# A fused forward-and-backward block on one Trainium2 core: the first stage gets a written order of loads and turns

## The chip, the cores and the metric

The kernel runs on one core of one Trainium2 chip. The metric is the device time of one execution in microseconds. A core has five engines with a queue each, which they work off in the order in which the program was built: TensorE (PE; its weight loads are listed apart, as PEld), VectorE (DVE), ScalarE (ACT), GpSimd (POOL) and SyncE (SP), which here only issues transfers. Transfers (DMA) run on 16 engines that all queues share; SP issues the plain and the transposing ones, POOL the gathers and most stores.

## What is computed

The reference is the forward pass of a block and all its gradients. Cut to what matters:

```python
mod = (_silu(c) @ w_mod).reshape(c.shape[0], 6, 1, -1)
sa, ca, ga, sb, cb, gb = (mod[:, 0], ..., mod[:, 5])
h = _layernorm(x) * (1 + ca) + sa
x = x + ga * irfft2(rfft2(h) * (w_r + 1j * w_i))      # spectral mixer
h = _layernorm(x) * (1 + cb) + sb
z = _layernorm(h)                                     # MLP
x = x + gb * (gelu(z @ w1 + b1) @ w2 + b2)
...
_out, _vjp = jax.vjp(_f, A_x, A_w_r, A_w_i, B_w1, B_b1, B_w2, B_b2, c, w_mod)
_grads = _vjp(grad_out)
```

There are 2048 tokens of width 1024, a hidden width of 3584, and all inputs are bfloat16. The backward pass of the MLP needs (grad_out * gb) @ w2^T, which depends on no forward result: only on grad_out, on the row gb and on w2. The kernel calls this product `ph`.

## The kernel before

The first stage has four jobs.

- Rows of `mod`. `mod_block(r, h)` makes half h of row r: eight products of 128x512 (line 278) over a 1 MB tile of w_mod that `mod_load` brings (line 270), and one eviction out of PSUM (line 281). Row 5 is gb, row 1 is ca, row 0 the shift sa; the rows 2, 3 and 4 (`late_mods`) are needed later. Their tiles take turns in three buffers.
- grad_out turned and scaled. `load_go(j)` loads a quarter of 512 tokens (1 MB, line 350). For each quarter and each of eight column chunks four 128x128 products against an identity fill a PSUM tile `pt` (line 386), which DVE (even chunks, line 390) or ACT (odd chunks, line 394) evicts into `gBoT[j]`, multiplied by the column `gb_col`. That column comes out of the gb row by eight tiny products (line 378) and one copy (line 380).
- The product `ph`. `ph_part(fc, js)` makes, for 128 hidden units fc and the token quarters js, eight products of 128x512 each over `wt` and `gBoT[j]` (line 808), and one eviction (line 814); a complete fc is stored by POOL (line 816). `wt` holds two tiles of w2^T; `load_w2t(fg)` brings one, for two values of fc, as a transposing transfer of 0.5 MB (line 341). There are 28 values of fc, so 896 products, the last 64 of them behind the first MLP products. They depend on nothing but gb, grad_out and w2, so TensorE works on them wherever something else isn't ready.
- The spectral mixer's input. `load_tok` loads a quarter of x by one plain transfer on SP (line 143) and two gathers on POOL (line 145), 0.25 MB each. Then DVE and ACT make the layer norm (`ln_dve`, `ln_mix`, `norm_act`: lines 487, 497, 501, 504, 512), and DVE scales by 1 + ca and folds (line 194, all through the helper `tt`). The first products on the folded input are `pu` (line 535). Beside this POOL, DVE and ACT make tables of sines (`gen_mats`, `trig`: index products on POOL, line 416; a reduction on DVE, line 443; the sine on ACT, line 444), into buffers of which one is grad_out's second quarter (`smb`) and one its first (`px1`).

In the kernel before the loads stand in the order in which the lines 358 to 375 name them: ca first, then gb, grad_out, the first w2 tile, the other quarters of grad_out and of x. The products of the four row halves, the turns of all four quarters and then `ph` follow each other. A scheduler that places instructions by its own estimates decides what lies between what on each engine; `tc.issue_after(x)` puts a floor under it (not before x), and `tc.high_priority()` lets an eviction go ahead. What is built is a fixed order per engine.

After the spectral mixer the kernel makes a second and a third layer norm per quarter (`consume_fwd`, stored as `d_n3` on line 865), while TensorE works through a long run of `ph` products. Then the MLP begins with the products `pz` (line 937), whose evictions are ACT's (line 940). From the first `pz` on the order on TensorE is the same in both kernels.

Of the kernel before, what the change touches and what calls it, by code (L numbers as in the profile page):

```python
# [17 lines left out]
P = 128  # L18
# [17 lines left out]
def kernel(  # L36
# [104 lines left out]
    def load_tok(t4, src, i, eng=None):  # L141
        s3 = tok_flat(src)
        ins = (eng or nc.sync).dma_start(out=tok_plain(t4, i), in_=tok_rows(s3, i, 0, D))
        for q in range(2):
            nc.gpsimd.indirect_dma_start(out=t4[:, tok_idx(i, q), :], out_offset=None, in_=s3,
                                         in_offset=bass.IndirectOffsetOnAxis(ap=xidx[:, 2 * i + q:2 * i + q + 1], axis=0))
        return ins
# [120 lines left out]
    def mod_load(r, h, wblk, eng):  # L268
        cb = 2 * r + h
        eng.dma_start(out=wblk, in_=w_mod[:, cb * KH:(cb + 1) * KH].rearrange("(j p) n -> p j n", p=P))  # L270

    def mod_block(r, h, wblk=None):
# [4 lines left out]
        for jc in range(NDC):  # L277
            nc.tensor.matmul(pm[:], lhsT=u_b[:, jc, :], rhs=wblk[:, jc, :], start=(jc == 0), stop=(jc == NDC - 1))
# [3 lines left out]
        if r in (1, 4):  # L282
            nc.vector.tensor_scalar(out=dst, in0=dst, scalar1=1.0, scalar2=None, op0=ALU.add)

# [64 lines left out]
    def load_go(j):  # L349
        nc.sync.dma_start(out=gos[j], in_=go_f[j * BW:(j + 1) * BW, :].rearrange("(a p) d -> p a d", p=P))  # L350
# [3 lines left out]
    def mod_get(r, h):  # L354
        wm[r, h] = mod_tile()
        mod_load(r, h, wm[r, h][:], nc.sync)

    mod_get(1, 0)
    load_tok(x4s[0], A_x, 0)
    mod_get(1, 1)  # L360
    mod_get(5, 0)
    for h in range(2):
        mod_block(1, h, wm[1, h][:])
    mod_get(5, 1)
    load_go(0)
    load_w2t(0)
    load_go(1)
    load_tok(x4s[1], A_x, 1)
    load_go(2)
    load_go(3)  # L370
    for h in range(2):
        mod_block(5, h, wm[5, h][:])
    load_tok(x4s[2], A_x, 2)
    load_tok(x4s[3], A_x, 3)
    load_w2t(1)
    pc = ps_d("pc")
    for cch in range(NDC):
        nc.tensor.matmul(pc[:, cch:cch + 1], lhsT=gb_row[0:1, cch * P:(cch + 1) * P], rhs=ones_bf[0:1, 0:1], start=True, stop=True)
    with tc.high_priority():
        nc.vector.tensor_copy(out=gb_col[:], in_=pc[:, 0:NDC])  # L380
    for j in range(4):
        for cch in range(NDC):
            pt = ps_f("pt")
            for a in range(4):
                q = (0, 2, 3, 1)[a] if j % 2 == 0 else (1, 3, 2, 0)[a]
                nc.tensor.matmul(pt[:, q * P:(q + 1) * P], lhsT=gos[j][:, a, cch * P:(cch + 1) * P], rhs=(ident, irev)[a // 2],
                                 start=True, stop=True)
            if cch % 2 == 0:
                with tc.high_priority():
                    nc.vector.tensor_scalar(out=gBoT[j][:, cch, :], in0=pt[:], scalar1=gb_col[:, cch:cch + 1], scalar2=0.0,  # L390
                                            op0=ALU.mult, op1=ALU.add, accum_out=gu[:, j, cch:cch + 1])
            else:
                with tc.high_priority():
                    nc.scalar.activation(out=gBoT[j][:, cch, :], in_=pt[:], func=ACT.Identity, scale=gb_col[:, cch:cch + 1],
                                         accum_out=gu[:, j, cch:cch + 1])
# [18 lines left out]
    def pts(out, in0, s1, s2, o0, o1=None):  # L414
        kw = {} if o1 is None else {"op1": o1}
        nc.gpsimd.tensor_scalar(out=out, in0=in0, scalar1=s1, scalar2=s2, op0=o0, **kw)
# [18 lines left out]
    def trig(dst, colv, rowv, nrow, width, modn, cosine):  # L435
# [3 lines left out]
        for r in range(nrow):  # L439
            ov = idx[:, r * width:(r + 1) * width]  # L440
            pts(ov.rearrange("p (s w) -> p s w", s=2) if len(colv.shape) == 3 else ov, colv, rowv[r], sh, ALU.mult, ALU.add)
# [3 lines left out]
                             bias=negpi[:], scale=2 * np.pi / modn)  # L445

# [4 lines left out]
    def gen_mats():  # L451
        for cl, colv, modn in ((CE, kev, 2048), (SE, kev, 2048), (CO, kod, 4096), (SO, kod, 4096)):
# [4 lines left out]
            for r in range(0, n, 2):  # L457
                trig(sm[:, cl // 2, r:r + 2, :], colv, rows[r:r + 2], 2, 512, modn, cl < 2)
            nc.gpsimd.dma_start(out=d_SF[:, cl, 0:n], in_=sm[:, cl // 2])
# [335 lines left out]
    pho = reg.tile([P, 3, 4, BW], BF16, name="pho", tag="ot")  # L795
    phs = [pho[:, k] for k in range(3)] + [reg.tile([P, 4, BW], BF16, name="phr", tag="ph")[:]]
    last_pe = [None]

    def ordered():
        return tc.issue_after(last_pe[0].ins)  # L800

    def ph_part(fc, js):
        fg, k = fc // 2, fc % 2
        ph2 = phs[fc % 4]
        for j in js:
            pp = ps_f("pp")
            for cch in range(NDC):
                last_pe[0] = nc.tensor.matmul(pp[:], lhsT=wt[:, fg % 2, cch, k * P:(k + 1) * P], rhs=gBoT[j][:, cch, :],  # L808
                                              start=(cch == 0), stop=(cch == NDC - 1))
            q = (0, 2, 3, 1)[j]  # L810
            ov = ph2[:, :, q * P:(q + 1) * P]
            pv = pp[:, :].rearrange("p (i w) -> p i w", w=P)
            with tc.high_priority():
                nc.any.tensor_copy(out=ov, in_=pv)  # L814
        if js[-1] == 3:
# [735 lines left out]
```

## Time and profile before

| what | before |
|---|---|
| median of 3 runs | 1419.64 us (1416.66 to 1420.49) |
| profiled execution, its own time | 1419.22 us |
| span of its profile | 1417.4 us |
| busy PE, DVE, ACT, POOL | 1367.5, 1071.1, 745.6, 377.1 us |
| bytes moved | 333.22 MB |
| granted TensorE clock, mean | 0.99 |

In a timeline row stand the start, the busy time, the engine and line, the operation with its output and inputs, the number of instructions merged in the row, and in brackets the idle time before it with what ended it. A windows row gives for one stretch the busy time of each engine with the instruction count, then the granted clock of TensorE, the mean busy share of the 16 DMA engines, and GB/s.

### The profile page before, as it was taken

How to read it: one execution, taken by the hardware profiler on the slowest of the kernel's cores; microseconds unless marked ns; L12 is line 12 of the kernel's file. 1: busy time of each engine (PE TensorE's matmuls, PEld its weight loads, DVE VectorE, ACT ScalarE, POOL GpSimd, SP SyncE). 2: the span in 40 equal slices, each digit the busy share in tenths (PEclk: the TensorE clock that was granted, in tenths of full speed). 3: DMA queues.
4: the chain of work that ended last, by engine and by line, in shares of the span. 5: the costliest groups of instructions: out<-in, count | busy, mean ns of one | idle time of the engine just before them, and what ended most of it. 6: DMA issues, size and time to landing. Idle time of an engine off the chain costs nothing. (4 is left out here: it accounts for less than half of the span.)

```text
span 1417.4 us, 18569 instructions
## 1 busy us (share of the span) xinstructions
PE 1367.5 (96%) x6839; PEld 663.0 (47%) x6963; DVE 1071.1 (76%) x1503; ACT 745.6 (53%) x1063; POOL 377.1 (27%) x479
## 2 busy tenths in 40 slices
PE   5999999999999999999999999999999999999998
PEld 2545675444444444444444444344544565444443
DVE  5898889987698877886520788999488659898642
ACT  4775667667887765666315583343623445343211
POOL 5500623201112122212210011011367432322332
PEclk8899999999999999999999999999999999999999
DMA  9972647899688776687999399996699997666993
GB/s 330 304 226 72 181 137 226 261 277 348 239 235 267 231 252 233 200 275 232 292 287 233 115 271 319 210 298 193 191 279 281 242 242 207 189 180 182 288 261 118
DMA packets 356689, 333.22 MB, mean 235 GB/s; under 512 B 207578, under 2 KB 297200, under 8 KB 356470
## 3 DMA queue, kind: packets, MB, share of 16 engines
q1 hardware_dynamic: 319110, 205.61, 55.1%
q0 software_dynamic: 37488, 126.42, 25.7%
q8 instruction: 54, 0.88, 0.3%
q14 instruction: 37, 0.30, 0.1%
HBM read 166.77 MB, written 115.92 MB: 199 GB/s over the span
## 5 line engine op out<-in xcount | busy, mean ns | idle before, releaser
L808 PE MATMUL pp<-gBoT,wt 128*128 128x512 bf16 x874 | 196.3, 381 | 4.0 <-DMA wt<-in_B_w_dram 2.8
L1094 PE MATMUL pg<-w1T,gzr 128*128 128x512 bf16 x877 | 195.0, 379 | 3.7 <-ACT gn3b L1109 1.7
L1445 PE MATMUL gw1acc<-gzh,n3n 128*128 128x512 bf16 x877 | 194.1, 379 | 1.0
L1094 PEld LDWEIGHTS <-gzr 128*128 128x128 bf16 x896 | 86.4, 98 | 110.8 <-issue 7.9
L808 PEld LDWEIGHTS <-wt 128*128 128x128 bf16 x896 | 87.6, 98 | 107.5 <-DMA wt<-in_B_w_dram 3.3
L937 PEld LDWEIGHTS <-w 128*128 128x128 bf16 x896 | 87.1, 98 | 107.4 <-issue 2.7
L1445 PEld LDWEIGHTS <-n3n 128*128 128x128 bf16 x896 | 87.2, 98 | 105.2 <-issue 1.3
L937 PE MATMUL pz<-n3Ta,w 128*128 128x512 bf16 x439 | 98.2, 379 | 1.8 <-ACT gt L940 1.3
L937 PE MATMUL pz<-n3Tb,w 128*128 128x512 bf16 x436 | 98.0, 379 | 0.7 <-issue 0.2
L940 ACT ACTIVATE gt<-pz,b_col 128x512 bf16<-128x512 f32 x112 | 73.5, 684 | 38.1 <-PE pz L937 37.6
L994 PEld LDWEIGHTS <-hhA 128*128 128x128 bf16 x608 | 58.9, 98 | 73.4 <-issue 3.0
L1227 PE MATMUL gw2acc<-gB,hhsA 128*128 128x512 bf16 x406 | 91.2, 379 | 0.5
L1449 ACT CAST gwo<-gw1acc 128x512 bf16<-128x512 f32 x49 | 28.5, 582 | 111.0 <-PE gw1acc L1445 103.2
L194 DVE TENSOR_TENSOR gt<-gt,gt 128x2048 bf16<-128x2048 bf16 x56 | 68.5, 1224 | 20.6 <-ACT gt L953 19.4
L951 ACT ACTIVATE gt<-gt 128x2048 bf16<-128x2048 bf16 x28 | 53.5, 1910 | 55.1 <-DVE gt L194 55.1
L194 DVE TENSOR_TENSOR ct<-ct 128x2048 bf16<-128x2048 bf16 x68 | 80.8, 1217 | 1.4 <-DMA d_n<-ct 0.5
L1234 ACT CAST gwo<-gw2acc 128x512 bf16<-128x512 f32 x46 | 26.7, 582 | 101.0 <-PE gw2acc L1227 83.2
L1227 PEld LDWEIGHTS <-hhsA 128*128 128x128 bf16 x416 | 40.6, 98 | 47.9
L947 ACT ACTIVATE gt<-gt 128x2048 bf16<-128x2048 bf16 x28 | 53.5, 1910 | 1.7 <-DVE w2sA L194 1.0
L1450 POOL DMA_DIRECT2D out_dram<-gwo x56 | 30.7, 549 | 88.6 <-ACT gwo L1449 66.2
L953 ACT ACTIVATE gt<-gt 128x2048 bf16<-128x2048 bf16 x28 | 53.4, 1908 | 0.4
L814 ACT CAST pho<-pp 128x512 bf16<-128x512 f32 x59 | 33.5, 582 | 32.4 <-PE pp L808 31.9
(346 smaller groups left out, 2544.5 us busy)
## 6 DMA issues: line engine op xcount, KB each, us to landing
gzr<-d_gz SPq DMA_DIRECT2D x28, 512.0 KB, 6.4
wblk<-in_w_mod_dram SPq DMA_DIRECT2D x12, 1024.0 KB, 8.8
out_dram<-otl POOLq DMA_DIRECT2D x48, 256.0 KB, 4.5
out_dram<-gwo POOLq DMA_DIRECT2D x96, 128.0 KB, 4.2
d_ph<-pho POOLq DMA_DIRECT2D x21, 512.0 KB, 5.6
d_hh<-hhA POOLq DMA_DIRECT2D x19, 512.0 KB, 5.0
w<-in_B_w_dram SPq DMA_DIRECT2D x7, 1024.0 KB, 11.7
hhC<-d_ph SPq DMA_DIRECT2D x14, 512.0 KB, 9.5
```

The costliest lines, as they stand in the source:

```text
L194: return nc.vector.tensor_tensor(out=out, in0=a, in1=b, op=op)
L808: last_pe[0] = nc.tensor.matmul(pp[:], lhsT=wt[:, fg % 2, cch, k * P:(k + 1) * P], rhs=gBoT[j][:, cch, :], start=(cch == 0), stop=(cch == ...
L814: nc.any.tensor_copy(out=ov, in_=pv)
L937: last_pe[0] = nc.tensor.matmul(pz[:], lhsT=w1s[g][:, cch, k * P:(k + 1) * P], rhs=n3T[:, cch, :], start=(cch == 0), stop=(cch == NDC - 1))
L940: z_in = nc.scalar.activation(out=zb[:, k, :], in_=pz[:], func=ACT.Identity, bias=b1_col[:, fc:fc + 1], scale=1.0)
L947: nc.scalar.activation(out=av, in_=zb, func=ACT.Square)
L951: nc.scalar.activation(out=sg, in_=bv, func=ACT.Sigmoid, scale=2.0 * GK)
L953: nc.scalar.activation(out=bv, in_=bv, func=ACT.Sigmoid, scale=-2.0 * GK)
L994: last_pe[0] = nc.tensor.matmul(pbs[i][:], lhsT=hh[:, k, i * P:(i + 1) * P], rhs=wp[:, k, :], start=False, stop=(g == 6 and k == 3))
L1094: last_pg[0] = nc.tensor.matmul(pgs[i][:], lhsT=gzs[b, g][:, k, i * P:(i + 1) * P], rhs=w1Ts[g][:, k, h * KH:(h + 1) * KH], start=(g == 0 ...
L1227: nc.tensor.matmul(acc[:], lhsT=hh_of(fc)[:, t, :], rhs=gBs[t // 4][:, t % 4, h * KH:(h + 1) * KH], start=(t == 0), stop=(t == NT - 1))
L1445: nc.tensor.matmul(acc[:], lhsT=n3ns[t // 4][:, t % 4, cch * P:(cch + 1) * P], rhs=gz2[t // 8][:, t % 8, :], start=(t == 0), stop=(t == NT ...
```

## The change

The loads, the products and two groups of DVE and ACT work in the first stage get a stated order by chains of `issue_after`.

```diff
-    mod_get(1, 0)
-    load_tok(x4s[0], A_x, 0)
-    mod_get(1, 1)
-    mod_get(5, 0)
...
+    for what in (("w", 5, 0), ("t", 0), ("w", 5, 1), ("g", 0), ("g", 1), ("x", 0), ("g", 2), ("g", 3),
+                 ("w", 1, 0), ("w", 1, 1), ("x", 1), ("t", 1), ("x", 2), ("x", 3)):
+        start_load(*what)
+    for step in ((mod_block, 5, 0), (mod_block, 5, 1), (pt_part, 0, range(4), held), (gb_turn,), (pt_part, 0, range(4, 8)),
+                 (pt_part, 1, range(4)), (ph_part, 0, (0,)), (pt_part, 1, range(4, 8)), (ph_part, 1, (0,)),
+                 (pt_part, 2, range(4)), (ph_part, 0, (1,)), (pt_part, 2, range(4, 8)), (ph_part, 1, (1,)),
+                 (pt_part, 3, range(4)), (ph_part, 0, (2,)), (pt_part, 3, range(4, 8)), (ph_part, 1, (2,)),
+                 (mod_block, 1, 0), (mod_block, 1, 1), (ph_part, 0, (3,)), (ph_part, 1, (3,))):
+        with ordered():
+            if step[0] is mod_block:
+                last_pe[0] = mod_block(step[1], step[2], wm[step[1:]][:])
+            else:
+                step[0](*step[1:])
...
+            if cl == SE:
+                for g in x_gather[0]:
+                    behind(g, ins)
+            ins = nc.gpsimd.dma_start(out=d_SF[:, cl, 0:n], in_=sm[:, cl // 2])
+            if cl in (SE, CO):
+                for g in x_gather[1] if cl == SE else x_gather[2] + x_gather[3]:
+                    behind(g, ins)
...
-    PH_EARLY = 6
+    PH_EARLY = 8
+    load_w2t(2)
+    for fc in range(2, PH_EARLY):
...
         if i == 0:
-            with tc.issue_after(u_in.ins):
+            with tc.issue_after(ev_v[1, 2].ins), tc.issue_after(ev_a[1, 7].ins):
                 ln_dve(x4, 0, i)
...
+        with tc.issue_after(ev_v[3, 6].ins):
+            scaled.append(tt(fb, fb, bcn(opca_row, 4), ALU.mult))
```

New are `start_load(what, ...)`, which issues one load behind the last ("w" a half row of w_mod, "t" a w2 tile, "g" a quarter of grad_out, "x" one of x), `pt_part(j, cs)`, which turns the chunks cs of quarter j, `gb_turn()`, which makes `gb_col` and then the evictions of the four tiles held back for it, and the lists `ev_v` and `ev_a` of the turns' evictions on DVE and ACT. Nothing is computed that was not computed before. A program's order is known when it is built; at the places that matter it is:

| queue | before | after |
|---|---|---|
| SP | ca half, x0, ca half, gb half, go0, gb half, w2 tile 0, go1, x1, go2, go3, x2, x3, w2 tile 1, shift halves | gb half, w2 tile 0, gb half, go0, go1, x0, go2, go3, both ca halves, x1, w2 tile 1, x2, x3, shift halves |
| POOL | the eight gathers of x, then the index products | index products for two tables, gathers of x0, a table store, an index product, a second store, gathers of x1, five index products, a store, gathers of x2 and x3, the rest |
| PE, products of 128x512 on `ph` ahead of the shift's row products / ahead of the second group of `pu` / in the run ahead of `pz` | 24 (6 more between the shift's halves) / 268 / 464 | 80 / 329 / 413 |
| DVE between `gb_col` and the last eviction of a turn | 16 turn evictions, 2 index reductions, 1 statistics pass | 16 turn evictions, 5 index reductions, 7 statistics passes of x0, 3 `ph` evictions |
| DVE ahead of the first scaling by 1 + ca | the shift's row is evicted later | both halves of the shift's row evicted and folded first |
| ACT ahead of the first `pz` eviction | all work on the third quarter's norms | three of the third norm's four passes on the third quarter; the last quarter's statistics ahead of the fourth `pz` eviction |

The line numbers of the profile before are those of the kernel before; in the kernel after `ph` is line 371, the turns 386, their evictions 396 and 399, the row products 280, `pu` 586 and `pz` 970.

148 lines of the change are left out of this document (78 added, 70 removed).

## The prediction

> **What bounds the kernel now.** I read the page first, then busy time by stage.
>
> ```profile
> span 1417.4 us, 18569 instructions
> ...
> PE 1367.5 (96%) x6839; PEld 663.0 (47%) x6963; DVE 1071.1 (76%) x1503; ACT 745.6 (53%) x1063; POOL 377.1 (27%) x479
> ```
>
> ```profile
> core 0: us, PE busy (x) PEld busy (x) DVE busy (x) ACT busy (x) POOL busy (x), PEclk, DMA share, GB/s
> ...
> 10.00:22.00 12.00, 5.72 (x21) 2.25 (x21) 5.49 (x17) 4.72 (x7) 8.76 (x17) 0.76 1.05 381
> ...
> 31.00:40.00 9.00, 6.48 (x56) 5.89 (x57) 5.98 (x15) 5.61 (x14) 0.00 (x0) 0.50 1.04 398
> ...
> 46.60:54.00 7.40, 7.40 (x36) 3.39 (x35) 7.40 (x12) 7.27 (x11) 5.89 (x6) 1.00 1.06 361
> 0.00:45.00 45.00, 25.51 (x170) 16.52 (x173) 25.11 (x70) 24.44 (x46) 22.13 (x52) 0.77 1.00 320
> 45.00:130.00 85.00, 79.89 (x390) 38.17 (x395) 77.57 (x115) 57.29 (x86) 23.56 (x28) 1.00 0.65 208
> 130.00:260.00 130.00, 128.25 (x789) 77.62 (x799) 117.16 (x162) 88.17 (x151) 47.73 (x42) 1.00 0.59 175
> 260.00:420.00 160.00, 155.09 (x702) 69.73 (x715) 131.00 (x166) 116.99 (x131) 27.59 (x34) 0.99 0.92 279
> ```
>
> TensorE sets the time: of 50 us in which it isn't busy, 19.5 lie in the first 45, where the transfers run without a gap (share 1.00) and no engine is busy for over 57%. That stage is bound by loads and their order. Next, TensorE's timeline and SP's.
>
> ```profile
> 6.20 3.41 PE L278 MATMUL pm<-wblk,u_b 128*128 128x512 bf16 x8 [3.61 <-DMA wblk<-in_w_mod_dram]
> 11.16 1.89 PE L278 MATMUL pm<-wblk,u_b 128*128 128x512 bf16 x8 [1.55 <-DMA wblk<-in_w_mod_dram]
> 18.17 3.59 PE L278 MATMUL pm<-wblk,u_b 128*128 128x512 bf16 x8 [5.12 <-DMA wblk<-in_w_mod_dram]
> ...
> 24.15 1.90 PE L278 MATMUL pm<-wblk,u_b 128*128 128x512 bf16 x7 [0.57 <-DMA wblk<-in_w_mod_dram]
> ...
> 31.06 3.76 PE L386 MATMUL pt<-ident,go 128*128 128x128 bf16 x32 [1.20 <-DMA go<-in_grad_out_dram]
> ...
> 44.43 5.34 PE L808 MATMUL pp<-gBoT,wt 128*128 128x512 bf16 x23
> ...
> 52.63 1.89 PE L278 MATMUL pm<-wblk,u_b 128*128 128x512 bf16 x8
> ```
>
> ```profile
> 11.13 12.82 SPq L341 DMA_TRANSPOSE wt<-in_B_w_dram  x1
> 24.01 0.57 SPq L350 DMA_DIRECT2D go<-in_grad_out_dram  x1
> ...
> 42.42 12.49 SPq L270 DMA_DIRECT2D wblk<-in_w_mod_dram  x5
> ```
>
> gb, the row everything else hangs on, is complete only at 26.05 (24.15 + 1.90); the first `ph` product starts at 44.43. From there TensorE is nearly full, so what it gains here stays, unless a later wait takes it back.
>
> ```profile
> 122.16 0.83 PE L535 MATMUL pu<-smA,fbuf 128*128 128x256 bf16 x6 [1.26 <-DVE fbuf L194]
> ...
> 220.27 86.28 PE L808 MATMUL pp<-gBoT,wt 128*128 128x512 bf16 x392
> 309.33 15.68 PE L808 MATMUL pp<-gBoT,wt 128*128 128x512 bf16 x62 [2.77 <-DMA wt<-in_B_w_dram]
> 324.84 7.07 PE L937 MATMUL pz<-n3Ta,w 128*128 128x512 bf16 x32
> 331.75 13.98 PE L808 MATMUL pp<-gBoT,wt 128*128 128x512 bf16 x62
> ```
>
> One 128x512 product costs (331.75 - 324.84) / 32 = 0.216 us, a `ph` part of eight 1.73.
>
> **The loads.** The w2 tile's issue ends at 23.95, when all ahead of it has drained (gb's last half is used from 24.15). The next load, go1, goes out at 24.01 and is used from 31.06: 7.05 us for tile and go1. At the 381 GB/s of 10 to 22 us go1's 1.05 MB take 2.75, so a tile takes 4.3. In the new order gb's first half is used at 6.2, as ca's was; the tile adds 4.3, gb's second half 2.75 (13.3), go0 16.0, go1 18.8, x0's plain half 20.2, go2 22.9, go3 25.7, ca 31.2. The gathers of x0 and x1 and the table stores (1.6 MB on POOL's queue) push the later ones back by up to 4.2.
>
> **The turns.** gb's second half takes 3.6 at the half rate of the row at 18.17, to 16.9. Behind it stand sixteen small turn products (1.8; 3.76 for 32 in the row at 31.06) and gb's column (about 1.0): evictions begin near 19.6. DVE's prices:
>
> ```profile
> 28.00 0.75 DVE L390 TENSOR_SCALAR_CACHE_REDUCE gBoT<-pt,gb_col 128x512 bf16<-128x512 f32 x1
> ...
> 28.67 0.75 DVE L390 TENSOR_SCALAR_CACHE_REDUCE gBoT<-pt,gb_col 128x512 bf16<-128x512 f32 x1
> ...
> 29.34 0.69 DVE L443 TENSOR_SCALAR gidx<-gidx 128x1024 int32<-128x1024 int32 x1
> ...
> 46.35 0.69 DVE L814 CAST pho<-pp 128x512 bf16<-128x512 f32 x1
> ...
> 47.27 1.28 DVE L497 BATCH_NORM_STATS2 st<-x 128x6 f32<-128x512 bf16 x2
> ```
>
> Start to start an eviction is 0.67, the others 0.6. Sixteen evictions make 10.8, five index reductions (one of half size) 2.8, seven statistics passes of x0 4.2, three `ph` evictions 1.8, small ones 0.4: 20.0, to 39.6. TensorE has 112 small products (13.2 at 0.117) and six `ph` parts (10.4): from 19.1 to 42.7; by DVE alone, whose last eviction one more part follows, 41.3. I take the later. Behind it stand ca's two halves (16 products, 3.5; their tiles are there by 35.4) and two `ph` parts (3.5): 49.7.
>
> New waits: DVE now meets x0 in the middle of the turns. Its first statistics pass is reached near 24.9 (19.6 + six evictions + two index reductions), x0's plain half lands at 20.2 to 24.4. Behind that pass are the evictions of go1, and TensorE's next turn waits for their PSUM. I price this wait at 0, and at 3 as a bound. The gathers, now behind index products on POOL, cost nothing: x0's go out near 10 us, and those of x1 to x3 are read only after the turns.
>
> **The shift's row.** Next come the two halves of the shift. Their loads stand behind the same bytes in both orders (both ca and gb halves, all of grad_out and x, two w2 tiles), and in both the transfers never pause. In the kernel before their issue begins at 42.42: 4.3 for the tile ahead and 2.9 each (1.05 MB at the 361 GB/s of 46.6 to 54) put the second at 52.5, and its product at 52.63 did not wait. So I take 54.5 (52.63 + 1.89) as their end in both kernels. Between 49.7 and there it has 3.8 us of products, so 1 us is idle (2.4 by DVE's pace): this hides a stage that is late by so much, and each us beyond costs one. At that end the old queue has 30 `ph` products behind it, the new one 80: 50 x 0.216 = 10.8 us ahead.
>
> **To the mixer.** Up to the second group of `pu`, TensorE then has 249 `ph` products against 238 (+2.4 us), and the row products are the same. It arrives at 122.16 - 1.26 (the wait for DVE) + 2.4 = 123.3, having made 61 x 0.216 = 13.2 us more work: 12.1 ahead. That holds if DVE has folded x by then.
>
> ```profile
> 49.06 2.41 DVE L194 TENSOR_TENSOR fbuf<-fbuf,rows 128x4096 bf16<-128x4096 bf16 x1
> ...
> 121.41 0.69 DVE L194 TENSOR_TENSOR fbuf<-fbuf,sb_saf 128x1024 bf16<-128x1024 bf16 x1
> ```
>
> ```profile
> L814 DVE CAST pho<-pp 128x512 bf16<-128x512 f32 x8 | 5.4, 679 | 0.0
> ...
> L814 DVE CAST phr<-pp 128x512 bf16<-128x512 f32 x3 | 2.0, 680 | 0.0
> ...
> L443 DVE TENSOR_SCALAR gidx<-gidx 128x512 int32<-128x512 int32 x4 | 1.7, 423 | 2.2 <-POOL gidx L416 2.2
> ```
>
> It took 73.0 from the first scaling to the end. In the new queue the shift's evictions and fold (2.7, about what they were inside) come first, so the scaling starts near 58 instead of 49. Inside fall out seven of the eleven `ph` evictions (4.2), the index reductions with their waits (4.2) and the shift (2.7); two statistics passes come in (1.2): 63, to 121. The cover is 2 us; I take 11.5 of the 12.1 (bounds 6, with the fold 6 late, and 13.2).
>
> **To the MLP.** The run of `ph` ahead of `pz` shrinks from 464 to 413 products, so `pz` could start near 313. Its wait of 2.77 for a w2 tile may go, since each tile is asked for a group of 64 products earlier: 0 to 2.8, I take 1. Against it, the mixer's results and the norms behind them don't come earlier.
>
> ```profile
> 310.99 2.37 ACT L512 ACTIVATE ct<-ct,stats 128x1024 bf16<-128x1024 bf16 x2 [1.72 <-DVE stats L194]
> ...
> 319.58 1.06 ACT L501 ACTIVATE ct<-xt 128x1024 bf16<-128x1024 bf16 x1 [0.86 <-DVE xt L194]
> ...
> 327.45 0.67 ACT L940 ACTIVATE gt<-pz,b_col 128x512 bf16<-128x512 f32 x1
> ```
>
> ACT makes the third quarter's passes from 310.99 and starts the last quarter's at 319.58; in its new queue these stand ahead of the first and the fourth eviction of `pz`. TensorE's PSUM tiles cover some. Nothing lost at the least, about 6 us at the most (319.58 + 2 against the fourth tile's end near 320, and the `ph` evictions that queue behind); I take 2.5.
>
> Sum: 11.5 + 1 - 2.5 = 10.0 off the profiled execution's own 1419.22 (the span's 1417.4 and 1.8 around it): 1409.2. The median lies 0.4 above that execution, so 1409.6; I say 1409.5. Behind `pz` the order on TensorE is the old one, and I add nothing.
>
> **Rivals.** *Given back at the MLP.* TensorE arrives 11 early at a chain of norms that hasn't moved, and waits for nearly all of it. For it: DVE is busy 131 of 160 us there, the transfers 92%. Against: `pz` needs only the first quarter, and the waits above have a bound of 6. With 10 lost: 1417. Chance 0.10.
>
> *The clock stays at half.* The turns pause again and again, and 31 to 40 us shows a granted clock of 0.50. Then eight products cost 3.41 instead of 1.89 (the rows at 6.20 and 11.16): 12.2 more for eight `ph` parts and 3.0 for ca, 15.2, of which 2 are hidden at the shift. Less the gain of 10 the end is 1422, or 1415 if half of them are hit. Against: at 44.43, right behind turns at half clock, 23 products took 5.34, close to full rate. Chance 0.07. The Trainium skill, "TensorE: Matmul & The Clock Gate", Part 1, has the clock at half by default and back there after an idle window of about 3.4 us, and at full after as long a busy one; by it, evictions that break up the turns could keep the gate shut, which no run yet shows.
>
> *Slower: a circle of in-order queues.* DVE's index reductions now stand between the turns' evictions. The one ahead of the last quarter needs POOL's index products, which stand behind four gathers, behind a table store that waits for ACT's sines, which wait for go1's turns on TensorE.
>
> ```profile
> 13.63 0.95 POOL L145 DMA_INDIRECT x<-in_A_x_dram,xu  x1 [0.31 <-issue]
> ...
> 41.09 1.48 POOL L416 TENSOR_SCALAR gidx<-genv 128x512 int32<-128x512 f32 x2 [12.16 <-ACT smB L444]
> ```
>
> By these prices (0.95 and 0.31 a gather, 0.74 an index product) POOL is through near 37, when DVE gets there. But POOL here waited 12.16 for one sine. If DVE, and with it TensorE, takes such a wait, the gain of 10 is gone at 12 us of delay (2 hidden); a second table follows, so two rounds bound it at 24, or 1431. I price it at one round and a third, 16: 1423 to 1424. Chance 0.15.
>
> The forecast keeps 0.68, with 1404 to 1414 as its own range.
>
> **How the numbers follow.** A change under 0.3% (4.3 us) can't be told from none here. Faster (below 1415.4): 0.68, 0.04 of the MLP rival and 0.03 of the clock's, so 0.75. Same: 0.10. Slower: 0.15. The range ends at 1403 (all bounds good: 13.2 + 2.8 off) and at 1420, which leaves out most of the slower case.
>
> **What would show it.** Right: the first `ph` part near 24 and eight done by 50; the shift's second half ending at 54 to 55; DVE's first scaling near 58; `pu`'s second group at 122 to 124; `pz` at 310 to 315; waits of 1 to 4 us right behind. Wrong: DVE idle ahead of an index reduction or of x0's statistics between 20 and 45; `pu` behind 126 with a wait for the fold; a `pz` past 320.

## The result and the profile after

| | before | after |
|---|---|---|
| median | 1420.07 us (1416.48 to 1422.62, 6 runs) | 1441.64 us (1431.15 to 1448.33, 6 runs) |
| ratio after / before | | 1.0147, 95% interval 1.0106 to 1.0188 |
| profiled execution, span | 1419.22, 1417.4 us | 1442.74, 1441.0 us |
| bytes moved | 333.22 MB | 333.22 MB |

The change makes the kernel 21.6 us slower; 10 us faster were forecast, and 1420 was the end of the range. The page of the kernel after:

```profile
span 1441.0 us, 18701 instructions
...
PE 1382.4 (96%) x6963; PEld 664.6 (46%) x6963; DVE 1071.3 (74%) x1506; ACT 743.2 (52%) x1059; POOL 372.5 (26%) x479
```

The work is the same (before's page lacks some 2% of TensorE's records), so what is lost is waiting, and products at a lower clock behind the waits. TensorE's timeline shows where:

```profile
21.43 2.58 PE L371 MATMUL pp<-gBoT,wt 128*128 128x512 bf16 x8
...
46.89 3.62 PE L371 MATMUL pp<-gBoT,wt 128*128 128x512 bf16 x16
54.96 3.60 PE L280 MATMUL pm<-wblk,u_b 128*128 128x512 bf16 x8 [4.45 <-DMA wblk<-in_w_mod_dram]
62.54 3.59 PE L280 MATMUL pm<-wblk,u_b 128*128 128x512 bf16 x8 [3.98 <-DMA wblk<-in_w_mod_dram]
...
134.32 0.83 PE L586 MATMUL pu<-smA,fbuf 128*128 128x256 bf16 x6 [2.30 <-DVE fbuf L196]
...
318.44 3.59 PE L371 MATMUL pp<-gBoT,wt 128*128 128x512 bf16 x8 [8.38 <-DMA wt<-in_B_w_dram]
325.98 14.25 PE L371 MATMUL pp<-gBoT,wt 128*128 128x512 bf16 x56 [3.94 <-DVE phr L377]
340.06 7.07 PE L970 MATMUL pz<-n3Ta,w 128*128 128x512 bf16 x32
...
411.43 8.75 PE L970 MATMUL pz<-n3Ta,w 128*128 128x512 bf16 x32 [4.58 <-ACT gt L973]
...
423.47 7.07 PE L970 MATMUL pz<-n3Tb,w 128*128 128x512 bf16 x32
```

The first `ph` part starts at 21.43 and all eight are done at 46.89 + 3.62 = 50.5: the turns went as forecast (49.7). Then the two halves of the shift wait for their loads and end at 66.1, not 54.5. `pu`'s second group is at 134.3 (before 122.16), so 12.2 late. `pz` is at 340.06 (before 324.84), 15.2 late although 51 fewer products stand in the run ahead of it: 8.38 went into a wait for a w2 tile and 3.94 into one for an eviction on DVE. By the first `pz` of n3Tb, 423.47, it is 20.7 (402.74 before, shown below), and at the end 23.6. So there are two places of loss, one at 50 to 66 us and one at 310 to 326, and a smaller one behind `pz`. DVE's timeline at both places:

```profile
58.59 0.69 DVE L283 CAST sar<-pm 128x512 bf16<-128x512 f32 x1 [7.35 <-PE pm L280]
...
70.16 2.28 DVE L196 TENSOR_TENSOR fbuf<-fbuf,rows 128x4096 bf16<-128x4096 bf16 x1
...
324.09 1.23 DVE L196 TENSOR_TENSOR ct<-ct 128x2048 bf16<-128x2048 bf16 x1 [16.31 <-DMA d_n<-ct]
```

DVE, behind TensorE in the same chain, idles 7.35 and 6.88 us for the shift, and its first scaling starts at 70.2 (forecast 58, before 49.06). Near 320 it waits 16.31 for the store of d_n, with a `ph` eviction queued behind. Both places lead to SP. Its timeline early, and then, first in the kernel after and then in the one before, around 300:

```profile
29.78 10.50 SPq L344 DMA_TRANSPOSE wt<-in_B_w_dram  x1
40.32 1.95 SPq L143 DMA_DIRECT2D x<-in_A_x_dram  x2
42.38 9.62 SPq L272 DMA_DIRECT2D wblk<-in_w_mod_dram  x3
```

```profile
285.66 13.84 SPq L955 DMA_TRANSPOSE n3Ta<-d_n  x1
299.69 1.13 SPq L912 DMA_DIRECT2D w<-in_B_w_dram  x2
300.91 14.17 SPq L344 DMA_TRANSPOSE wt<-in_B_w_dram  x1
315.27 0.44 SPq L912 DMA_DIRECT2D w<-in_B_w_dram  x1
315.80 1.34 SPq L898 DMA_DIRECT2D d_n<-ct  x1
```

```profile
281.87 4.38 SPq L922 DMA_TRANSPOSE n3Ta<-d_n  x1
...
290.08 0.90 SPq L879 DMA_DIRECT2D w<-in_B_w_dram  x1
292.77 8.78 SPq L341 DMA_TRANSPOSE wt<-in_B_w_dram  x1
```

The second column is how long the issue stood at the head of the queue. Early, the transposing load of w2 tile 1 holds it for 10.50 us, and x2, x3 and the shift's halves stand behind. That alone is no difference, since the same tile holds it as long in the kernel before:

```profile
31.73 10.59 SPq L341 DMA_TRANSPOSE wt<-in_B_w_dram  x1
```

The difference is in the transfers, shown below.

Late, n3Ta's load holds the queue for 13.84, w1 tiles (`w`) follow, and w2 tile 12, the one that TensorE waits for, comes to the head at 300.91. The store of d_n, which frees DVE, comes out only at 315.80, behind that tile. In the kernel before, the same loads stand ahead of the tile in the same order: n3Ta's, then two of w1. But there n3Ta's holds the queue for 4.38 only. SP's waits name a store of `ct` (9.1 us, ended at 294.73) as what n3Ta's load waited for. I don't read that as a wait for its buffer, since 254 of the load's 4096 packets of 256 B had gone by then, the first at 292.2. What it shows instead is a slow transfer. The two transposing loads, w2 tile 11 and n3Ta's, move in 281.3 to 287.6 before and in 283.8 to 303.6 after. What the queues moved in the seven us from 281, before, and in the seven from 291, after:

```profile
q1 hardware_dynamic: 6176, 1.57, 108.7%
q0 software_dynamic: 90, 0.30, 12.6%
```

```profile
q0 software_dynamic: 480, 1.77, 69.4%
q1 hardware_dynamic: 1120, 0.28, 45.2%
```

q1 is SP's queue and q0 POOL's; the columns are packets, MB and share of the engines. Before, SP's queue moves 1.57 MB in that time; after, 0.28, while POOL's queue moves 1.77. Between 293 and 294 each queue moves 93 packets, POOL's of 4 KB and SP's of 256 B: one for one, and so 0.38 MB against 0.02.

What does tile 1 do early? Its packets move from 36.6 to 45.6 after, and from 39.9 to 43.8 before. The transfers of the two us from 42 on, after and before:

```profile
DMA packets 519, 0.19 MB, mean 97 GB/s; under 512 B 503, under 2 KB 503, under 8 KB 519
...
q1 hardware_dynamic: 499, 0.13, 90.6%
q0 software_dynamic: 20, 0.07, 24.6%
```

```profile
DMA packets 1600, 0.42 MB, mean 211 GB/s; under 512 B 1574, under 2 KB 1600, under 8 KB 1600
...
q1 hardware_dynamic: 1600, 0.42, 99.7%
```

Undisturbed, q1 moves 0.42 MB in 2 us, nearly all of it the tile's packets of 256 B. After, it moves 0.13, while only 20 packets of POOL's gathers and stores are begun. I call this the crawl: a transposing load that moves far fewer packets than it can.

### The profile page after: what moved, and what is told of

Read it like the earlier page. It is cut to its first block, busy times and chain, and to the rows that moved or that the text cites. A ratio compares the mean times of both kernels' runs of the same rounds, so it can differ in the third digit from the quotient of the medians.

```text
span 1441.0 us, 18701 instructions
## 1 busy us (share of the span) xinstructions
PE 1382.4 (96%) x6963; PEld 664.6 (46%) x6963; DVE 1071.3 (74%) x1506; ACT 743.2 (52%) x1059; POOL 372.5 (26%) x479
## 2 busy tenths in 40 slices
DMA packets 356689, 333.22 MB, mean 231 GB/s; under 512 B 207578, under 2 KB 297200, under 8 KB 356470
## 5 line engine op out<-in xcount | busy, mean ns | idle before, releaser
L371 PE MATMUL pp<-gBoT,wt 128*128 128x512 bf16 x896 | 204.9, 388 | 13.4 <-DMA wt<-in_B_w_dram 8.4
L196 DVE TENSOR_TENSOR ct<-ct 128x2048 bf16<-128x2048 bf16 x68 | 81.0, 1219 | 17.3 <-DMA d_n<-ct 16.3
L973 ACT ACTIVATE gt<-pz,b_col 128x512 bf16<-128x512 f32 x112 | 73.3, 684 | 38.9 <-PE pz L970 38.5
L196 DVE TENSOR_TENSOR gt<-gt,gt 128x2048 bf16<-128x2048 bf16 x56 | 68.5, 1223 | 20.7 <-ACT gt L986 19.6
L377 ACT CAST pho<-pp 128x512 bf16<-128x512 f32 x53 | 30.6, 580 | 66.8 <-PE pp L371 66.7
```

The costliest lines, as they stand in the source:

```text
L196: return nc.vector.tensor_tensor(out=out, in0=a, in1=b, op=op)
L973: z_in = nc.scalar.activation(out=zb[:, k, :], in_=pz[:], func=ACT.Identity, bias=b1_col[:, fc:fc + 1], scale=1.0)
```

## The experiments

Two theories for the early loss. *A:* the tile crawls because POOL's transfers (gathers of x2 and x3, table stores, `ph` stores), moved to this time by the change, run beside it. *B:* it is the place in SP's queue: the shift's loads stand behind the tile, x2 and x3, and what is moved up to them is no longer the same as before. For the late loss: *C,* n3's load and the w1 loads ahead of the w2 tile in SP's in-order queue; its rival, that it is only the early delay carried on. The kernels start from the one after, if nothing else is said.

**e1, the shift's products later.** The row products go behind the `ph` part of fc 3; the loads stay.

```diff
-    for h in range(2):
-        mod_block(0, h)
     gen_mats()
...
+        if fc == 3:
+            with tc.issue_after(last_pe[0].ins):
+                for h in range(2):
+                    mod_block(0, h)
```

> The kernel after, with the shift's two row halves made behind 64 more ph products. Theory (the first loss is TensorE waiting for the shift's loads, which land at 62.5, and nothing else): the two waits of 4.5 and 4.0 us and the half-rate products (3.4) go, pu's second group starts at 121 to 123 instead of 134.3, DVE's first scaling near 52. If the second loss ahead of pz stays as it is, the time falls by 11 to 12 us, to about 1430. Rival (what is gained here is lost again ahead of pz, where a fixed chain ends): pu at 121 to 123, but pz still near 340 and a time within 4 us of 1441. Rival (DVE, not the loads, is the limit): pu stays behind 130 with a wait for the fold.

1433.85 us, 1.0101 [1.0049, 1.0153]: 15.1 above its before. The shift doesn't wait any more, but `ph` now waits for the crawling tiles themselves, 3.20 and 8.21 us, and `pu` is at 133.33. Late, the tile's wait is there as in after, 8.80 us. Moving the consumer shows that the transfers are late, not the order on TensorE; tile 1's packets took 15.6 us here.

**e2, n3's load one tile later.**

```diff
-            with tc.issue_after(w2ts[11].ins) if b == 0 else ExitStack():
+            with tc.issue_after(w2ts[12].ins) if b == 0 else ExitStack():
```

> The kernel after, with the transposing load of n3 put one w2 tile later in SP's queue; the order on all other engines is unchanged. Theory (the second loss is SP's queue: n3's load waits 9.1 us for a store that frees its buffer, and the w2 tile and the d_n store behind it go out late): TensorE's wait of 8.4 us for the w2 tile near 310 falls below 3, DVE's wait of 16.3 us for the d_n store below 5, pz starts at 327 to 330 instead of 340.1, the time falls by 9 to 12 us to about 1431. Rival (the transfers are simply full there, share 1.11): the waits stay above 6 us and pz behind 336, the time within 4 us of 1441.

1440.59, 1.0169 [1.0131, 1.0207]: no gain. The wait of 8.38 went to the next and last w2 tile (8.88, ended at 330.40), `pz` stayed at 340.20. n3's load alone is not the cause; the w1 loads still stood there.

**e3, three of POOL's stores behind the shift.** The stores of `ph` 0 and 1 and of the table d_E.

```diff
+    for k in (0, 1, "E"):
+        behind(ph_store[k], shift_in)
```

> The kernel after, with three stores on POOL's queue (two of ph, one table, 2.1 MB) put behind the shift's second row product; the order on all other engines is unchanged. Theory A (their bytes delay the shift's loads, 2.1 MB at 385 GB/s are 5.4 us): the shift's second half ends at 60 to 62 instead of 66.1, TensorE's two waits fall from 8.4 to 3 to 4 us, pu at 129 to 130. Theory B (the loads are late because they stand behind x and because one of them waits for ca's buffer): the end moves by less than 2 us.

1440.45, 1.0138 [1.0095, 1.0181]. The shift came later still (one wait of 16.06, to 65.39): tile 1's packets took 18.0 us, from 35 to 53, with the gathers of x2 and x3 and another table store beside it. The three stores are not what makes it crawl; the rest of A is open here.

**e4, the shift's loads ahead.** Both loads right behind ca's, the second half into a part of `fbuf` that is free then.

```diff
-                 ("w", 1, 0), ("w", 1, 1), ("x", 1), ("t", 1), ("x", 2), ("x", 3)):
+                 ("w", 1, 0), ("w", 1, 1), ("w", 0, 0), ("w", 0, 1), ("x", 1), ("t", 1), ("x", 2), ("x", 3)):
...
-        mod_block(0, h)
+        mod_block(0, h, wm[0, h][:])
```

> The kernel after, with the shift's two loads right behind ca's in the stated order and the second one in a buffer that nothing holds (a quarter of fbuf); the loads of x1 to x3 and the second w2 tile come 5.5 us later. Theory (place in the queue and ca's buffer make them late): the shift's products follow the two ph parts without a wait and end at 54 to 55 at full clock, pu at 122 to 124, the time 8 to 12 us lower. Rival (the same bytes only change places): TensorE waits as long, 6 us or more in all, for the second w2 tile behind the shift, or DVE for x1, and pu stays behind 130.

1429.92, 1.0075 [1.0049, 1.0101]: 11.2 above its before, so half of the loss is gone. TensorE's timeline:

```profile
48.11 1.89 PE L282 MATMUL pm<-wblk,u_b 128*128 128x512 bf16 x8
49.99 1.89 PE L282 MATMUL pm<-fbuf,u_b 128*128 128x512 bf16 x8
...
128.88 0.83 PE L588 MATMUL pu<-smA,fbuf 128*128 128x256 bf16 x6 [1.83 <-DVE fbuf L196]
...
306.45 8.08 PE L373 MATMUL pp<-gBoT,wt 128*128 128x512 bf16 x24 [6.61 <-DMA wt<-in_B_w_dram]
```

No wait, and full rate: the shift ends at 51.9, 2.6 ahead of the forecast, and DVE's first scaling starts at 55.57. So the prediction's condition at the shift is more than met, and still `pu` is at 128.9 and not 123.3, waiting for the fold. The late wait (6.61) is there too.

**e5, POOL's queue cleared.** The gathers of x2 and x3 and two table stores go behind the last index product.

```diff
-            if cl in (SE, CO):
-                for g in x_gather[1] if cl == SE else x_gather[2] + x_gather[3]:
+            if cl == SE:
+                for g in x_gather[1]:
...
+            elif cl in (CO, SO):
+                held_back.append(ins)
...
+        for g in held_back:
+            behind(g, ins)
```

> The kernel after, with POOL's queue kept clear beside the second w2 tile: the gathers of x2 and x3 and two table stores (2.0 MB) stand behind the last index product; the orders of SP and TensorE are unchanged, and the same bytes are moved. Theory (a transposing tile crawls while POOL's queue has packets in flight: 200 to 500 small packets in 2 us beside them in the kernel after, 1570 without them in the kernel before; the shift's loads stand behind the tile): the tile is through by about 42, TensorE's waits for the shift fall from 8.4 to below 2 us, the second half ends at 54 to 56 instead of 66.1, pu's second group at 123 to 127, the time 8 to 11 us below the kernel after. Rival (place in the queue and ca's buffer alone make them late): the second half still ends behind 62 and the time moves by less than 4 us.

1437.01, 1.0145 [1.0114, 1.0176]. The timeline, and the two us in the tile:

```profile
47.91 1.89 PE L280 MATMUL pm<-wblk,u_b 128*128 128x512 bf16 x8
58.65 3.35 PE L280 MATMUL pm<-wblk,u_b 128*128 128x512 bf16 x8 [8.85 <-DMA wblk<-in_w_mod_dram]
```

```profile
DMA packets 1618, 0.49 MB, mean 243 GB/s; under 512 B 1577, under 2 KB 1577, under 8 KB 1617
```

With POOL's transfers away the tile is through in 3.9 us and the first half is on time. But the held-back transfers then run beside the second half, which waits 8.85: the shift ends at 62.0. So POOL's transfers beside SP's loads cost the shift about 8 us of the 11.6, crawl or no crawl.

**e6, n3 and the w1 tiles later.** e2's edit, and the w1 loads behind the w2 tiles (the list gives how many go behind each of the last w2 tiles).

```diff
-            load_w1((0, 2, 1, 4)[max(fc // 2 - 10, 0)])
+            load_w1((0, 0, 1, 6)[max(fc // 2 - 10, 0)])
```

> The kernel after, with n3's transposing load one w2 tile later in SP's queue (as in the run before this) and the first w1 tiles behind it: none, none, one and six at the last four w2 tiles instead of none, two, one and four. All other engines keep their order. Theory (the w2 tiles stand behind n3's load and 3 MB of w1 in one in-order queue): TensorE's longest wait for a w2 tile between 290 and 340 falls from 8.4 to below 4 us, pz starts at 328 to 332 instead of 340.1, the time is 7 to 11 us below the kernel after. Rival (the wait only moves on to another load, as it did with n3's load alone): a wait of 6 us or more for a w2 tile, n3 or w1 stays, the time within 4 us of 1441.

1428.77, 1.0092 [1.0063, 1.0121]: 9.8 above its before. The timeline:

```profile
316.75 7.08 PE L371 MATMUL pp<-gBoT,wt 128*128 128x512 bf16 x32 [0.92 <-DMA wt<-in_B_w_dram]
323.67 7.07 PE L970 MATMUL pz<-n3Ta,w 128*128 128x512 bf16 x32
```

The tile's wait falls from 8.38 to 0.92, and `pz` is at 323.67. The early order is after's; in this execution tile 1 did not crawl (4.6 us), the shift still waited and ended at 62.5, and `pu` was at 130.30, 4.0 earlier than in after. Nor did n3Ta's load, at its later place: its packets took 4.6 us, against 11.4 in after. The other 12.4 us of the 16.4 at `pz` were gained between `pu` and `pz`.

**e7, e5 and e6 together.**

> Both edits of the two runs above together. If the two losses are separate, their gains add: pu at 123 to 127, pz at 316 to 322, a time of 1420 to 1425, the kernel before's. If the second loss is that of an early TensorE at a fixed chain (the mixer's results and the norms), pz stays at 326 or later and the time at 1429 or more.

1425.85, 1.0055 [1.0028, 1.0081]; `pu` at 129.49, `pz` at 323.48. **e8, e4 and e6 together:**

> The shift's loads early (the fourth run: 1429.9, pu at 128.9, a wait of 6.6 us for a w2 tile ahead of pz) with n3's load and the first w1 tiles later. Separate losses: the wait of 6.6 falls below 3, the time 4 to 8 us below 1429.9. A fixed chain: pz waits in the tile's place, the time within 3 us of 1429.9.

1423.87, 1.0033 [1.0013, 1.0052]: 4.9 above, so 16.7 of the 21.6 are gone (the two gains, 10.4 and 11.8, overlap). Its `pz` was no earlier than e6's, for a new wait:

```profile
315.09 10.35 PE L373 MATMUL pp<-gBoT,wt 128*128 128x512 bf16 x40 [10.67 <-DVE phr L379]
```

TensorE waits 10.67 for a `ph` eviction on DVE, and DVE in turn for the store of d_n (12.54, ended at 313.21).

**e9, e8 with the `ph` evictions from fc 22 on ACT; e10, those of fc 2 to 7 too.** The edit is e10's; e9's has `fc >= 22` alone.

```diff
-                nc.any.tensor_copy(out=ov, in_=pv)
+                (nc.scalar.copy if fc >= 22 or 2 <= fc < 8 else nc.any.tensor_copy)(out=ov, in_=pv)
```

> The run before with early shift loads and late w1 loads (1423.9), with the evictions of ph from fc 22 on all on ACT. There TensorE lost 10.7 us behind evictions that stood on DVE behind a wait for a d_n store (12.5 us). Theory (what is still missing is this wait, and TensorE's lead is real): that wait falls below 3 us, pz starts at 315 to 319 instead of 325.3, the time is 1413 to 1418, below the kernel before. Rival (the lead is worth nothing, since n3, the first w1 tiles and the norms end where they ended): pz stays behind 322, or waits for ACT's gt and the norms grow by as much, and the time stays within 4 us of 1423.9.

> The kernel of the run beside this one, with the evictions of ph for fc 2 to 7 on ACT too. Theory (pu and all norms behind it hang on DVE's fold, and DVE has 99 us of work ahead of it whatever the order): pu's second group starts 2 to 5 us earlier than 128.3, and the time is 1 to 4 us below that run. Rival (ACT becomes late instead, with 78 of 128 us busy there): waits for ACT's evictions of 2 us or more ahead of pu, and no gain.

e9: 1440.42, 1.014 [1.0117, 1.0163]. e10: 1420.79, 1.0027 [1.0011, 1.0043]. In the late stretch their queues are nearly the same, and yet the same w2 tile stood at the head of SP's queue for 14.00 us in the one and for 3.81 in the other:

```profile
298.95 14.00 SPq L346 DMA_TRANSPOSE wt<-in_B_w_dram  x1
```

```profile
297.88 3.81 SPq L346 DMA_TRANSPOSE wt<-in_B_w_dram  x1
```

Ahead of it stands n3Ta's load, whose packets took 15.2 us in e9 and 4.4 in e10. In the four us from 288, e9 and then e10, SP's queue moved:

```profile
q1 hardware_dynamic: 2218, 0.57, 117.5%
```

```profile
q1 hardware_dynamic: 3934, 1.01, 115.4%
```

POOL's queue began no packet in those four us of either. So the crawl strikes here too, and without POOL's transfers: theory A can't be all of it. e10 also shows what a lead at `pz` can come to. Its timeline, and a row of the kernel before:

```profile
311.79 7.07 PE L972 MATMUL pz<-n3Ta,w 128*128 128x512 bf16 x31
...
363.19 8.75 PE L972 MATMUL pz<-n3Ta,w 128*128 128x512 bf16 x32 [4.32 <-ACT gt L975]
...
391.35 8.47 PE L972 MATMUL pz<-n3Ta,w 128*128 128x512 bf16 x32 [5.80 <-ACT gt L975]
...
403.12 7.07 PE L972 MATMUL pz<-n3Tb,w 128*128 128x512 bf16 x31
```

```profile
402.74 6.85 PE L937 MATMUL pz<-n3Tb,w 128*128 128x512 bf16 x31
```

e10 starts `pz` 13.0 us ahead of before (324.84), in the window that I forecast, and 91 us later it is 0.4 behind. Two waits for ACT's `gt` took 10.1, and 3.1 went into products at a lower clock behind them (8.75 and 8.47 against 7.07). e10 has also given ACT more to do ahead of `pz`, so this is not a clean test of the lead.

**e11, e6's edit in the kernel before.**

> The kernel before, with n3's transposing load one w2 tile later and the first w1 tiles later, as in the kernel after it brought 12.9 us. Theory (the queue ahead of pz is a loss that the change brought, since its w2 tiles meet n3's load and w1 at another moment): the kernel before, which waits 2.8 us there, gains at most 2 us and stays within 4 us of 1419. Rival (a fault of both kernels): 5 us or more faster.

1417.47, 1.0006 [0.9979, 1.0034]: nothing that can be told. The old kernel has the same order and loses 2.77 by it, so it is not the order that the change brought but the slow loads in it. The profiled execution, the fastest of its ten, starts `pz` at 319.06 and `pz` of n3Tb at 396.96: 5.8 ahead of before at both, so here a lead at `pz` was kept. **e12, the w1 half of e6 alone:**

> The kernel after, with only the first w1 tiles later (none, none, one and six), n3's load in its old place. n3's load moved alone brought 1 us, both together 12.9. If the w1 bytes ahead of the w2 tile are the whole cause: 1427 to 1432, and no wait for a w2 tile above 4 us. If n3's wait of 9 us for its buffer holds up the queue as well: 1434 to 1439, a wait of 3 us or more left for the w2 tile near 310.

1433.67, 1.009 [1.0058, 1.0121]. `pu` is at 130.31, as in e6, and `pz` at 331.92 with waits of 3.93 and 3.82 left, against e6's 323.67. After's `pz` is at 340.06 with a `pu` 4.0 later, so of the 12.4 us that e6 gains between `pu` and `pz` the w1 tiles alone give 4.1; n3's load alone gives nothing (e2, where it took 12.1 us at its new place), and only both clear the queue. C holds, with two kinds of load in it; what makes it cost more than before is n3Ta's slow load.

**e13, go0 on POOL's queue from the start, beside w2 tile 0.** A test of A.

```diff
+            elif what == "g" and a[0] == 0:
+                nc.gpsimd.dma_start(out=gos[0], in_=go_f[0:BW, :].rearrange("(a p) d -> p a d", p=P))
```

> The kernel after, with the first quarter of grad_out (1 MB) loaded by POOL's queue from the start instead of SP's, so that it moves beside the first w2 tile, which in the kernel after runs alone (about 2000 small packets from 5 to 8 us). Theory (POOL's packets make a transposing tile crawl): fewer than 500 small packets per us while they flow, tile and quarter together take 8 us or more instead of 3 and 2.8, gb's second half is used at 16 or later instead of 11.98. Rival (queues only share the bandwidth): the two are through in 6 us, the small packets stay above 600 per us in most of it, gb's second half is used by 14.8 at the latest.

1441.60, 1.0155 [1.013, 1.0181]. gb's second half was used from 14.95, against 11.98 in after: less than A asked (16 or later), more than its rival (14.8 at the latest). The tile ran undisturbed; POOL's packets and the tile's shared hardly a microsecond, so A was not put to the test.

**e14, e10 with x1's plain load ahead of the shift's.**

```diff
-                 ("w", 1, 0), ("w", 1, 1), ("w", 0, 0), ("w", 0, 1), ("x", 1), ("t", 1), ("x", 2), ("x", 3)):
+                 ("w", 1, 0), ("w", 1, 1), ("x", 1), ("w", 0, 0), ("w", 0, 1), ("t", 1), ("x", 2), ("x", 3)):
```

> The kernel of e10 with the plain load of x1 ahead of the shift's two loads; no other queue changes. There DVE waited 2.3 us for x1 and then 2.8 for ACT's norm behind it. Theory (the end follows DVE's fold, not TensorE's lead): both waits shrink, pu's second group starts 2 to 4 us earlier than 128.0, pz no more than 2 earlier than 311.8, and the time falls by 2 to 4 us below 1420.8, to 1417 to 1419. Rival (the end follows TensorE's work): pu 2 to 4 earlier and the time within 1 us of 1420.8.

1419.88, 1.0022 [1.0008, 1.0035]. `pu` came at 126.10, 1.9 earlier than in e10, but `pz` at 317.56 behind a w2 wait of 4.50: not told apart from e10 in time.

**e15, e16, e17: three more overlaps, one execution each.** e13 with the tile behind both gb halves; e5 with the gathers of x2 and x3 released ahead of tile 1; e5 with the table stores left in their old place.

> As e13 (grad_out's first quarter on POOL's queue from the start), with the first w2 tile behind both of gb's halves, so that the tile begins near 8 to 9 us, when POOL's quarter flows (7 to 11 us in e13). Theory (any transfer of POOL's queue makes a tile crawl): fewer than 500 small packets per us while the two overlap, and the tile takes 6 us or more for its 2048 packets instead of 3. Rival (a plain load only shares the bandwidth): the tile is through within 5 us, with over 600 small packets in most of them.

> e5 with the four gathers of x2 and x3 back in front, issued near 25 to 30 us, and both large table stores still late. If gathers make the second tile crawl: 100 to 500 small packets per us beside them between 34 and 46, instead of 700 to 900 in e5. If they don't, or are through before it begins: the tile is moved within 4 us at 600 packets per us or more, as in e5.

> e5 with the two large table stores back in front (near 27 and 36 us) and the gathers still late. If stores make the second tile crawl: fewer than 500 small packets per us while one flows, and a tile that takes 6 us or more. If not: within 4 us, as in e5.

1434.22, 1433.12 and 1437.26, beside 1420.49 for the kernel before. In e15 POOL's quarter of grad_out had flowed before the tile began, and in e16 the gathers had: both tiles came to some 1000 small packets per us. But e16's moved only 312 in the two us from 37, and POOL's queue none. In e17 a store met the tile at 39 to 40: 155 small packets beside POOL's 5 in one us, 661 beside 43 in the next, and the tile took 5 to 6 us instead of 4. None made the tile in question crawl as long as after's; e15's tile 1, at its old place, took 11.0 us. That POOL's transfers slow a transposing load fits e5, n3Ta's load and after, and is not proved by these; e9 and e16 have slow stretches without them, and what starts a crawl and how long it lasts stays open.

## Why the prediction was wrong

*Right.* **The loads** and **The turns**: eight `ph` parts done at 50.5, 49.7 forecast. The new waits there are small, the largest 1.22 on TensorE, and DVE's longest wait ahead of an index reduction is 2.12, where the slower rival took 16: *a circle of in-order queues* did not happen, and that the end is on its side is no credit to it. *The clock stays at half* did not happen either: `ph` parts among the turns took 1.89 from the second on. But behind the waits the clock fell: the shift's halves took 3.60 and 3.59 behind 4.45 and 3.98 of idle time, at a granted clock of 0.50, and 1.89 each in e4 without them. That is 1.7 for each wait, which no term held.

*Wrong first: "The shift's row".* I wrote that the same bytes stand ahead in both orders and that the transfers never pause, hence 54.5 in both. 66.1 was measured, and these 11.6 cover the shortfall at `pu` (134.3 for 123.3). The step failed on the bytes and on the rate. Up to the shift's second half SP's queue moves the same, 14.0 MB before and 14.3 after, but POOL's moves 3.1 before and 5.8 after, and in all they come to 17.3 MB (to 53 us) and about 20.1: two `ph` stores and a table store (2.1 MB) now fall in that time. And a busy share near 1 is no rate: tile 1 held 90.6% of the engines and moved 0.13 MB in 2 us. The second half also has to wait for ca's tile, into which it loads (its issue goes out at 45.36). That cost nothing that I can see, since tile 1 was still being moved and x2, x3 and the first half stood ahead. By size: about 3.6 are the crawl, about 8 POOL's transfers beside SP's loads. Four profiles have after's first stage. Where tile 1 took 9.0 and 8.0 us (after, e2), the shift ends at 66.1 and 65.3 and `pu` is at 134.3 and 133.6; where it took 4.6 and 5.2 (e6, e12), it ends at 62.5 and `pu` is at 130.3. The 8 are what is left then (62.5, and e5's 62.0, against 54.5); 1.7 of them are the last wait's price in clock. e4, whose loads stand ahead of the tile and of those stores, removes it all.

*Wrong second: "To the mixer".* I had DVE's fold take 63 from the first scaling. Windows of that stretch, and from the start to `pu`, in before, after and e4 (busy PE, PEld, DVE, ACT, POOL with counts; the third pair is DVE's):

```profile
49.06:122.16 73.10, 68.00 (x311) 30.36 (x315) 69.59 (x98) 47.36 (x70) 21.40 (x25) 1.00 0.68 215
```

```profile
70.16:134.32 64.16, 61.60 (x285) 27.68 (x284) 62.15 (x80) 37.59 (x57) 8.76 (x11) 1.00 0.52 163
```

```profile
55.57:128.88 73.31, 69.96 (x313) 31.06 (x312) 66.10 (x89) 45.23 (x71) 12.12 (x13) 0.95 0.69 205
0.00:128.88 128.88, 109.08 (x567) 51.27 (x567) 99.48 (x178) 78.57 (x126) 44.05 (x82) 0.97 0.83 257
```

In after it took 64.2, close to my 63, but only because the late shift had let other work go first. In e4, where the shift is on time, it took 73.3: DVE had 66.1 of work there, 3.5 less than before and not the 7.7 that I had taken out (that sum is 4.2 of evictions, 2 of the 4.2 for the index reductions, 2.7 of the shift, less 1.2), and 7.2 of idle time. Groups of DVE's instructions in e4's stretch show one cause (busy, mean ns, idle before and its releaser):

```profile
L379 DVE CAST pho<-pp 128x512 bf16<-128x512 f32 x5 | 3.5, 691 | 4.1 <-PE pp L373 4.1
```

Five `ph` evictions stand in DVE's queue ahead of the folds and wait 4.1 for products that TensorE had not made yet. The term was 10 too small. Up to `pu` DVE has 99.5 of work, and a fold at 121 would have left it 22 of idle time; by the first scaling of e4 alone it had idled 22.2 (55.57 less 99.48 - 66.10). With the shift as forecast `pu` would have come near e4's 128.9, 6.7 later than before with 13.2 us more work done: a lead of 6.5, next to my lower bound of 6.

*Wrong third: "To the MLP".* I gained 1 there because each tile is asked for a group earlier. It is not. `wt` holds two tiles, so a tile can be asked for only when TensorE is through with the last but one: before, tile 12's issue begins at 292.77, the 13.8 us of one tile's 64 products ahead of the end of the run at 306.6. After, that moment is 296.3 (310.07 less 13.8), but n3Ta's load holds the queue until 299.50 and two w1 loads are moved ahead of the tile: 8.38 and 3.94 lost, against before's 2.77. e6, which puts both kinds of load behind the tile, takes 11.8 off (21.6 above its own before in after, 9.8 in e6). I had taken the loads of that stretch at the speed that they had before; n3Ta's took 11.4 us for 3.8, beside POOL's transfers. Why these now meet it there was not tried. `pz` at 340.06, forecast 310 to 315: of the 27 us, 11.0 are `pu`'s and 12.3 the two waits; 2.2 went in the mixer (100.26 us from `pu` to the run for 98.11) and the rest I don't place.

*Wrong fourth: "Behind `pz` ... I add nothing".* I took 2.5, at most 6, for ACT's norms ahead of the evictions of `pz`. In after 5.5 more are lost by the first `pz` of n3Tb, 4.58 of them in the wait for `gt`: within that bound. But e10, with the faults of the loads mended, loses its whole lead of 13 there. *Given back at the MLP* named this loss and got 0.10: the kernel arrives early at a chain (norms, d_n, ACT's evictions) that has not moved as far. It made 1417 in that rival; e10's 1420.79 is that case with a little more lost. Whether the forecast's 10 could have been kept is not shown: e10 lost its lead with more work on ACT, and e11's execution kept 5.8. No kernel here beat the one before beyond what can be told: e11 is at 1.0006 of it, e14 at 1.0022.

## What to carry to other kernels

"Same bytes ahead" gives the time of a load only if the other queues move the same beside it, the buffer is free, and the share of busy engines goes with the same GB/s. So ask of every load that something waits for not only what stands ahead of it in its own queue, but what the other queues move at that time, to the end of the stretch that changes. At a slow issue, look at the packets before you name its cause: here the same order cost 2.8 us in one kernel and 12.3 in the other. And a lead can be lost at the next chain that did not move: e10's 13 us at `pz` were nothing 91 us later, e11's 5.8 were kept.

## What the runs showed of the hardware

A transposing load moves in packets of 256 B, and its speed varies widely. From its first packet to its last, w2 tile 1 (0.5 MB) took 3.7 to 5.6 us in thirteen of the 19 profiles, and 8.0 in e2, 9.0 in after, 9.9 in e13, 11.0 in e15, 15.6 in e1 and 18.0 in e3. n3Ta's load (1 MB) took 3.8 to 4.6 us in the four profiles with fewer than 30 of POOL's packets beside it (before, e6, e7, e10) and 8.0 to 23.8 in the other fifteen, with 80 to 1054.

I counted over the profiles, up to 330 us, the stretches of a microsecond in which SP's queue begins 50 or more packets of 256 B and few others. Their median is 688 where POOL's queue begins none, 368 beside 5 to 15 of POOL's, 344 beside 16 to 40 and 190 beside more. Part of that is mere sharing, packet by packet: where POOL's packets of 4 KB flow without a pause, the engines can move one of SP's for each of them (93 and 93 between 293 and 294 in after; 249 and 254, 1.41 and 0.25 MB, between 56 and 60). The rest is not explained, as e9's and e16's slow stretches without POOL's packets show.

The engines count as busy all the while (90.6% in after, while the tile moved at 64 GB/s). The Trainium skill, "DMA: Bandwidth & Descriptors", Latency and other measured facts, gives 261 GB/s for a transposing transfer whose rows are not contiguous: the free tile's 201 (1574 packets in 2 us) and the 288 of n3Ta's load in before lie on either side of it, and the crawling tile's 64 is not explained by it.

The same order of transfers did not give the same rate: after, e2, e6 and e12 have one order in the first stage, and the tile crawled in two of them; e9 and e10 agree in the late one, and their issue took 14.00 and 3.81. That is a likely reason for the wide spread of after (17.2 us in 6 runs against 6.1 before), not a shown one, since only one execution of each has a trace.
